# The second MLP product by Strassen's scheme, and a last h batch in five PSUM buffers

## The chip, the cores and the metric

The kernel runs on one core of one Trainium2 chip. The metric is the device time of one execution in microseconds; smaller is better. The engines are called by the names of the profile: PE is TensorE's matmul, PEld its weight load, DVE is VectorE, ACT is ScalarE, POOL is GpSimd and SP is SyncE, which here issues the DMAs.

## The reference

Attention over 8 batches and 8 heads (576 tokens, head dimension 64) in which scores more than tau below the row's maximum are dropped, followed by a two-layer MLP on the 4,608 tokens.

```python
scores = scale * np.matmul(q, k.transpose(0, 1, 3, 2))
thresh = np.max(scores, axis=-1, keepdims=True) - tau
scores = np.where(scores >= thresh, scores, -1000000000.0)
attn = softmax(scores)
x = (attn @ v) as tokens x 512                    # 4608 x 512
h = x @ w_in                                      # 4608 x 2048
g = h * np.tanh(softplus(h))                      # Mish
return (g @ w_out).astype(np.float32)             # 4608 x 512
```

## The kernel before

The kernel works on transposed data: tokens are columns. Products that need more than one pass of precision split each float32 operand into an upper part (a copy to the fp32r type, on ACT) and a lower part (the difference, on DVE or POOL), and add three products: upper x upper, upper x lower, lower x upper. So every block of the MLP costs three matmuls.

**Attention.** A loop over 288 tiles (`g`), nine per pair of heads, makes scores, softmax, transposes and the product with the values. Between its steps PE is given pieces of the first MLP product of the batch before: `gemm1` (line 455) is a generator that yields after each matmul, and `advance` (line 485) takes as many as a table says. The 32 blocks of `w_in` and the upper half of `w_out`'s columns are decoded in the same loop: the weights arrive as 64-bit words and become float32 by two ACT instructions, three DVE instructions and one POOL addition (`Decode`, lines 115 to 154). The decoded upper half of `w_out` goes back to HBM as `w2d`. All compute engines run strictly in the order in which the program is written (`InOrder`, line 81); DMAs are issued by SP.

**First product, last batch.** Each of the 16 blocks `f` of 128 features and both halves `c` of 288 tokens make one tile `h`: 12 matmuls of 288 columns. A finished tile is copied to `hst`, and four of them go to HBM (`hd`). The `h` tiles have two PSUM buffers (`psh`, line 164). For the last batch, which runs alone, lines 477 to 480 copy odd `f` on ACT and even `f` on DVE. During it the other half of `w_out` is loaded, decoded and split (`decode_step`, line 693), in part on POOL (line 705); the first chunk's `h` is read back, Mish is applied and the result is split, on POOL (`gate` at line 732); and `w2d` is read back and split (lines 739 to 743).

**Second product.** From line 767 on, ten chunks of tokens (256, eight times 512, 256) are multiplied by all of `w_out`: per chunk four blocks `d` of 128 outputs, each with 16 x 3 matmuls into one PSUM bank `o`, which DVE copies to `ost` for the output DMA. `make_g` (line 751) prepares the chunk after the next: load `h`, Mish and cast on ACT, subtraction on DVE. Engines other than PE are not held to the written order here, since line 749 takes the plain engines again.

Of the kernel before, what the change touches and what calls it, by code (L numbers as in the profile page):

```python
# [7 lines left out]
U32 = mybir.dt.uint32  # L8
# [29 lines left out]
NC = 512  # L38
PACE = {(5 * f) // 4: f for f in range(NF)}
GATES = (12, 15, 18, 21)  # L40
SPLITS = (24, 26, 28, 30)
CHUNKS = (0, *range(256, B * S, NC), B * S)
# [72 lines left out]
class Decode:  # L115


    def __init__(self, nc, st, hi, lo):
# [3 lines left out]
        self.c = self.words[:, :, 0]  # L122

# [23 lines left out]
    def add(self):  # L147
        self.nc.gpsimd.tensor_tensor(self.a, self.b, self.c, ALU.add)
# [4 lines left out]
    def lower(self, engine):  # L153
        engine.tensor_tensor(self.lo, fv(self.a), fv(self.hi), ALU.subtract)


def attention_moe(tc, q, k, v, tau, w_in, w_out, out):
# [3 lines left out]
    with ExitStack() as outer:  # L161
# [13 lines left out]
        with ExitStack() as first:  # L175
# [5 lines left out]

            with ExitStack() as att:
# [4 lines left out]
                dec = att.enter_context(tc.tile_pool(name="dec", bufs=5, side="right"))  # L187
# [3 lines left out]
                def skip():  # L191
                    pass

# [6 lines left out]
                def decode_w1(d, j):  # L200
                    sl = slice(j * WC, (j + 1) * WC)
                    st = dec.tile([P, 4 * WC], U32, name="dec")
# [12 lines left out]
                def decode_w2(f):  # L215
                    st = dec.tile([P, 4 * WC], U32, name="dec")
# [238 lines left out]
                def gemm1(b, xs):  # L455
# [88 lines left out]
                for g in range(NT + 5):  # L544
# [103 lines left out]
            wr = second.enter_context(tc.tile_pool(name="wr", bufs=1, side="right"))  # L648
            pso = second.enter_context(tc.tile_pool(name="pso", bufs=4, space=PSUM))

            def slot(pool, shape, kind, n):

                return pool.tile(shape, kind, name="g", tag="g", bufs=n)

            def small(kind, shape):
                return wr.tile(shape, kind, name="ht", tag="ht", bufs=2)

            def load_h(ht, c, fs):

                at, end = CHUNKS[c], CHUNKS[c + 1]  # L660
                while at < end:
                    i, off = divmod(at, HB)
                    m = min(HB - off, end - at)
                    to = at - CHUNKS[c]
                    nc.sync.dma_start(ht[:, :, to:to + m], hd[i][:, fs, off:off + m])
                    at += m

            def gate(ht, gh, gl, engine):
                nc.scalar.activation(ht, ht, AF.Mish)  # L669
                nc.scalar.copy(gh, ht)  # L670
                engine.tensor_tensor(gl, ht, fv(gh), ALU.subtract)  # L671

            def quarter(k):
                return slice(4 * k, 4 * k + 4)

            def weights2(pool, j):
                return [pool.tile([P, NF, WC], F32R, name=f"w2{n}{j}") for n in "hl"]

            n0 = CHUNKS[1]
            w2 = [weights2(wr, 0)]  # L680
            homes = []
            for _ in range(2):
                four = slot(wr, [P, 4, 4 * WC], U32, 4)
# [147 lines left out]
```

## Time and profile before

| | us |
|---|---|
| median of three runs | 1410.03 |
| the runs | 1406.82, 1410.03, 1417.41 |
| span of the profiled execution | 1404.3 |
| attention and the first seven batches (to the first matmul of the last batch) | 932.8 |
| last batch of the first product | 70.0 |
| second product, to the last instruction | 401.4 |

The span counts from the first to the last instruction of the profiled execution; no other time of that execution is shown, and the runs lie 2.5 to 13.1 us above it. In the rows, a matmul's duration contains the pipeline's end, which the next matmul overlaps; how fast PE streams is read from the distance of starts. Line 91 is the helper of the strict order, through which most instructions are recorded, so groups are told apart by tiles.

### The profile page before, as it was taken

The numbers are of one execution on the slowest core, as the hardware profiler recorded it, in microseconds if no ns is written. First come the engines' busy times: TensorE is split into PE (matmuls) and PEld (weight loads), VectorE is DVE, ScalarE is ACT, GpSimd is POOL, SyncE is SP. The second block draws the span as 40 slices with busy tenths as digits, with TensorE's granted clock in tenths as the row PEclk, the third lists the DMA queues.
The fourth block names the chain that finished last, engine by engine and source line by source line (L and its number), as shares of the span: only waits on it lengthen the run. The fifth ranks groups of instructions, "written<-read, shape, count | busy, mean of one in ns | idle before, by whom it ended". The sixth has DMA issues, their size and how long they took to land.

```text
span 1404.3 us, 27561 instructions
## 1 busy us (share of the span) xinstructions
PE 1364.3 (97%) x8798; PEld 1226.7 (87%) x8798; DVE 996.7 (71%) x2970; ACT 948.0 (68%) x2102; POOL 770.0 (55%) x1101
## 2 busy tenths in 40 slices
PE   8998899999999999999999999997999999999999
PEld 5555899999999999999999999997888888888888
DVE  5999999999999989999999999957433222322210
ACT  5878788888888888888888888856555333433310
POOL 4778888878788788787887878735200000000000
PEclk8999999999999999999999999999999999999999
DMA  4333333324333233333332333136555334543210
GB/s 141 97 101 107 116 125 111 120 90 130 98 117 109 92 123 119 102 112 103 104 119 91 117 95 108 63 133 237 162 161 144 111 112 120 143 113 113 83 53 30
DMA packets 124479, 158.81 MB, mean 113 GB/s; under 512 B 23472, under 2 KB 103344, under 8 KB 124336
## 3 DMA queue, kind: packets, MB, share of 16 engines
q1 hardware_dynamic: 124336, 157.07, 36.9%
q8 instruction: 70, 1.15, 0.3%
q14 instruction: 73, 0.60, 0.1%
HBM read 107.74 MB, written 49.28 MB: 112 GB/s over the span
## 4 chain that ended last, share of the span: by engine, by line
PE 84%; DVE 7%; ACT 5%; issue 2%; DMA 1%; POOL 0%; SPq 0%; ACTq 0%; DVEq 0%
PE o L780 28%; PE h L91 23%; PE s L91 13%; PE y L91 11%; PE tp L91 8%; DVE p L91 2%; DVE dec L91 1%; DVE st L91 1%; PE t L91 1%; DVE g L91 1%; ACT e L91 1%; ACT hi L91 1%; DVE lo L91 1%; DMA hd<-hst 1%; DVE tk L91 1%
## 5 line engine op out<-in xcount | busy, mean ns | idle before, releaser
L780 PE MATMUL o<-g,w2h 128*128 128x512 f32 (+1 forms) x1280 | 364.2, 370 | 0.7 <-ACT g L91 0.7
L91 PE MATMUL h<-xh,w1h 128*128 128x288 f32 x1024 | 304.8, 298 | 11.0 <-DVE hst L91 8.5
L91 PE MATMUL h<-xl,w1h 128*128 128x288 f32 x1024 | 304.1, 297 | 0.5 <-POOL xl L91 0.5
L91 PE MATMUL h<-xh,w1l 128*128 128x288 f32 x1024 | 303.8, 297 | 0.0
L91 POOL TENSOR_SCALAR p<-p,st 128x576 f32<-128x576 f32 x288 | 243.8, 846 | 62.4 <-DVE st L91 42.7
L91 PE MATMUL s<-k,q 128*128 128x288 f32 (+1 forms) x1280 | 257.7, 327 | 19.7 <-DVE p L91 17.0
L780 PEld LDWEIGHTS o<-g,w2h 128*128 128x128 f32 x1280 | 231.4, 188 | 44.5 <-ACT g L91 0.9
L91 ACT ACTIVATE e<-s,st 128x576 f32<-128x576 f32 x288 | 214.1, 744 | 55.0 <-DVE st L91 49.8
L91 DVE SCALAR_TENSOR_TENSOR p<-s,st,e 128x576 f32<-128x576 f32 x288 | 235.1, 816 | 21.3 <-ACT e L91 10.3
L780 PE MATMUL o<-g,w2l 128*128 128x512 f32 (+1 forms) x640 | 236.5, 370 | 0.0
L91 PEld LDWEIGHTS s<-k,q 128*128 128x128 f32 (+1 forms) x1280 | 184.2, 191 | 55.6 <-DVE p L91 36.6
L91 DVE TENSOR_REDUCE st<-s 128x1 f32<-128x576 f32 x288 | 216.6, 752 | 7.0 <-PE s L91 7.0
L91 PEld LDWEIGHTS h<-xh,w1h 128*128 128x128 f32 x1024 | 194.3, 190 | 13.5 <-DVE hst L91 10.2
L91 DVE TENSOR_TENSOR lo<-tp,hi 128x512 fp32r<-128x512 f32 (+1 forms) x280 | 174.2, 630 | 43.0 <-ACT hi L91 37.1
L91 PEld LDWEIGHTS h<-xl,w1h 128*128 128x128 f32 x1024 | 194.2, 190 | 0.9 <-POOL xl L91 0.9
L91 PEld LDWEIGHTS h<-xh,w1l 128*128 128x128 f32 x1024 | 194.2, 190 | 0.0
L671 DVE TENSOR_TENSOR g<-ht,g 128x1024 fp32r<-128x1024 f32 (+1 forms) x68 | 78.4, 1162 | 148.8 <-ACT g L670 148.8
L91 PE MATMUL tp<-ident,p 128*128 128x128 f32 x1152 | 175.0, 275 | 3.6 <-DVE lo L91 2.4
L91 ACT CAST hi<-tp 128x512 fp32r<-128x512 f32 (+1 forms) x280 | 149.8, 546 | 33.4 <-PE tp L91 30.0
L669 ACT ACTIVATE ht<-ht 128x1024 f32<-128x1024 f32 (+1 forms) x68 | 68.6, 1009 | 128.9 <-DMA ht<-hd 126.0
L91 PEld LDWEIGHTS tp<-ident,p 128*128 128x128 f32 x1152 | 139.0, 140 | 14.3 <-issue 7.3
L780 PEld LDWEIGHTS o<-g,w2l 128*128 128x128 f32 x640 | 120.5, 188 | 22.0
(64 smaller groups left out, 2196.5 us busy)
## 6 DMA issues: line engine op xcount, KB each, us to landing
hd<-hst SPq DMA_DIRECT2D x64, 576.0 KB, 3.3
r<-q SPq DMA_DIRECT2D x120, 160.0 KB, 2.4
r<-k SPq DMA_DIRECT2D x120, 160.0 KB, 2.3
ht<-hd SPq DMA_DIRECT2D x60, 288.0 KB, 3.3
r<-v SPq DMA_DIRECT2D x56, 160.0 KB, 2.3
dec<-w_in SPq DMA_DIRECT2D x32, 256.0 KB, 2.8
out_t<-ost SPq DMA_DIRECT2D x32, 256.0 KB, 2.2
dec<-w_out SPq DMA_DIRECT2D x16, 256.0 KB, 2.9
```

Of the source, the lines that this page charges most:

```text
L91: made = method(*args, **kwargs)
L669: nc.scalar.activation(ht, ht, AF.Mish)
L671: engine.tensor_tensor(gl, ht, fv(gh), ALU.subtract)
L780: nc.tensor.matmul(o[:, :m], a, b, start=n == 0, stop=n == 3 * NF - 1)
```

## The change

**The scheme.** The second product is cut into groups of 512 tokens, nine in all. Weights, features and tokens are each halved: `a` blocks of `w_out` (256 outputs x 1,024 features) and `b` blocks of Mish(h) (1,024 features x 256 tokens). Seven products of such blocks replace eight, by this form of Strassen's scheme (the first index of `a` is the output half and that of `b` the feature half):

- sums of weights, made once: s1 = a21 + a22, s3 = a11 - a21, s2 = a22 - s3, s4 = a12 - s2; seven weight blocks are split into upper and lower parts and stay in SBUF;
- sums of features, for each group: t1 = b12 - b11, then b12 becomes t3 = b22 - b12, b11 becomes t2 = t3 + b11, b21 becomes t4 = b21 - t2;
- products in this order, each 48 matmuls of 256 columns: a12 b21 into bank Y, a11 b11 into X, s1 t1 into Z, s2 t2 onto X, s4 b22 onto Z, a22 t4 into Y, s3 t3 onto X; between them banks are copied by ACT and added in the stores by DVE.

Each of the seven right operands is split after the sums (`operand`: four pieces, a cast on ACT and a subtraction on DVE), two products ahead, into a ring of 13 pieces. POOL does no subtraction any more. The strict order stays in force to the end. Lower halves, sums and splits of the weights are placed by number of the `h` tile (`at(u, ...)`) into the last batch; those of s2 and s3 lie in the first group.

**The last batch.** Its `h` tiles rotate over five PSUM buffers, two old ones and three new (`psx`); all are copied by ACT; `hst` has three buffers and is sent in two halves. Five of the sixteen pieces of `w_out`'s first output half are decoded in the last steps of the attention loop, and four more are loaded there.

```diff
+PIECE = (*range(8, 16), *range(8))
+EARLY = 284
...
                     for c, fs in order:
                         for f in fs:
-                            h = psh.tile([P, 512], F32, name="h", tag="ph")
+                            if b < B - 1 or f % 5 < 2:
+                                h = psh.tile([P, 512], F32, name="h", tag="ph")
+                            else:
+                                h = psx.tile([P, 512], F32, name="hx")
...
                             if f % 4 == 0:
-                                hst = xpool.tile([P, 4, HB], F32, name="hst", bufs=2)
-                            if b < B - 1 or f % 2:
-                                nc.scalar.copy(hst[:, f % 4], h[:, :HB])
-                            else:
-                                nc.vector.tensor_copy(hst[:, f % 4], h[:, :HB])
-                            if f % 4 == 3:
-                                nc.sync.dma_start(hd[2 * b + c][:, f - 3:f + 1, :], hst)
+                                hst = xpool.tile([P, 4, HB], F32, name="hst", bufs=3)
+                            nc.scalar.copy(hst[:, f % 4], h[:, :HB])
+                            n = 4 if b < B - 1 else 2
+                            if f % n == n - 1:
+                                nc.sync.dma_start(hd[2 * b + c][:, f + 1 - n:f + 1, :], hst[:, (f + 1 - n) % 4:f % 4 + 1])
...
+                    if EARLY <= g < EARLY + 9:
+                        decoding.extend(filter(None, [decode_top(g - EARLY)]))
...
+            halves = (slice(0, 4), slice(4, 8))
+            def split(raw):
+                made = [units.take(F32R) for _ in "hl"]
+                ups = [lambda s=s: nc.scalar.copy(made[0][:, s], raw[:, s]) for s in halves]
+                downs = [
+                    lambda s=s: nc.vector.tensor_tensor(made[1][:, s], raw[:, s], fv(made[0][:, s]), ALU.subtract)
+                    for s in halves
+                ]
+                return made, ups, downs
+            def combine(to, x, y, op):
+                return [lambda s=s: nc.vector.tensor_tensor(to[:, s], x[:, s], y[:, s], op) for s in halves]
...
+            def mish(raw):
+                for s in halves:
+                    nc.scalar.activation(raw[:, s], raw[:, s], AF.Mish)
+            def operand(raw):
+                parts = []
+                for i in range(4):
+                    s = slice(2 * i, 2 * i + 2)
+                    hl = ring.take(F32R)
+                    nc.scalar.copy(hl[:, 0], raw[:, s])
+                    nc.vector.tensor_tensor(hl[:, 1], raw[:, s], fv(hl[:, 0]), ALU.subtract)
+                    parts.append(hl)
+                return parts
+            r21, r22 = units.take(F32), units.take(F32)
+            for raw, at in ((r21, 0), (r22, 8)):
+                nc.sync.dma_start(raw, w2d[:, at:at + 8])
...
+            for n in range(5, 16):
+                at(n - 5, lambda n=n: coming[n - 5].first())
+                at(n - 4, lambda n=n: piece(n))
...
+            at(3, *a12u)
+            at(12, *a12d)
+            at(13, sum1)
+            at(14, split_into("s1", s1), lambda: units.give(s1))
...
-                if u in GATES:
-                    k = GATES.index(u)
-                    gate(h0[k], *(g[:, quarter(k)] for g in g0), nc.gpsimd)
...
-                    (nc.vector if k % 2 else nc.gpsimd).tensor_tensor(lo, raw2[:, quarter(k)], fv(hi), ALU.subtract)
+                for work in todo.pop(u, []):
+                    work()
                 advance(stream, UNIT)
...
-        nc = tc.nc
...
-                for f in range(NF):
-                    wh, wlo = (w[:, f, at:at + P] for w in w2[j])
-                    gh, gl = (x[:, f % 4] for x in g[f // 4])
-                    for a, b in ((wh, gh), (wh, gl), (wlo, gh)):
-                        nc.tensor.matmul(o[:, :m], a, b, start=n == 0, stop=n == 3 * NF - 1)
+        def multiply(a, b, o, first, last):
+            n = 0
+            for k in range(8):
+                gh, gl = (b[k // 2][:, i, k % 2] for i in range(2))
+                for m in range(2):
+                    wh, wlo = (w[:, k, m * P:(m + 1) * P] for w in a)
+                    for w, g in ((wh, gh), (wh, gl), (wlo, gh)):
+                        nc.tensor.matmul(o[:, m], w, g, start=first and n == 0, stop=last and n >= 45, skip_group_check=True)
                         n += 1
...
+        def store(pair, dh, th, x, y):
+            ost = small("ost", 4)
+            nc.vector.tensor_tensor(ost, x, y, ALU.add)
...
+        for pair in range(NPR):
+            nxt = {}
+            for i in range(7):
+                more = pair + 1 < NPR
+                if i == 0:
+                    if pair:
+                        store(pair - 1, 1, 1, X, tmp["p5"])
+                        store(pair - 1, 1, 0, X, tmp["y4"])
+                    else:
+                        mish(r["b22"])
+                    ops_.append(operand(r["t1"]))
+                    run_all(combine(r["b12"], r["b22"], r["b12"], ALU.subtract))
+                if i == 1:
+                    tmp["ysb"] = copied("ysb", Y)
+                    run_all(combine(r["b11"], r["b12"], r["b11"], ALU.add))
+                    ops_.append(operand(r["b11"]))
+                    if pair == 0:
+                        split_into("s2", r22)()
...
+                if i == 2:
+                    store(pair, 0, 0, X, tmp["ysb"])
+                    ops_.append(operand(r["b22"]))
+                    run_all(combine(r["b21"], r["b21"], r["b11"], ALU.subtract))
+                if i == 3:
+                    tmp["p5"] = copied("p5", Z)
+                    ops_.append(operand(r["b21"]))
...
+                    if pair == 0:
+                        split_into("s3", r21)()
...
+                if i == 5:
+                    tmp["zsb"] = copied("zsb", Z)
+                    store(pair, 0, 1, X, tmp["zsb"])
...
+                if i == 6:
+                    tmp["y4"] = copied("y4", Y)
+                    if more:
+                        mish(nxt["b12"])
+                        ops_.append(operand(nxt["b11"]))
+                        nxt["t1"] = units.take(F32)
+                        run_all(combine(nxt["t1"], nxt["b12"], nxt["b11"], ALU.subtract))
+                        mish(nxt["b22"])
+                name, o, first, last = (
+                    ("a12", Y, True, True), ("a11", X, True, True), ("s1", Z, True, True), ("s2", X, False, True),
+                    ("s4", Z, False, True), ("a22", Y, True, True), ("s3", X, False, True),
+                )[i]
+                multiply(A[name], ops_.pop(0), o, first, last)
+            r = nxt
...
-    nc = bacc.Bacc("TRN2", target_bir_lowering=False, num_devices=1)
+    nc = bacc.Bacc("TRN2", target_bir_lowering=False, num_devices=1, dynamic_dma_scratch_size=1024)
```

More of the change, by code (lines that the diff above doesn't have):

```diff
@@ L37 @@
 NBLK = 2 * B
[L38 to L42, printed above, removed]
+TC = 256
+PIECE = (*range(8, 16), *range(8))
+EARLY = 284
 QCOL = {
@@ L154, in lower, with __init__, add, take @@
         engine.tensor_tensor(self.lo, fv(self.a), fv(self.hi), ALU.subtract)
+class Homes:
+    def __init__(self, name, shape):
+        self._name, self._shape, self._pools, self._at = name, shape, [], {}
+    def add(self, pool, n, tag=None):
+        self._pools.append([pool, n, n, tag or self._name])
+    def take(self, kind):
+        home = next(h for h in self._pools if h[1])
+        home[1] -= 1
+        t = home[0].tile(self._shape, kind, name=self._name, tag=home[3], bufs=home[2])
+        self._at[id(t)] = (home, t)
+        return t
+    def give(self, t):
+        self._at.pop(id(t))[0][1] += 1
 def attention_moe(tc, q, k, v, tau, w_in, w_out, out):
@@ L180, in attention_moe, with home @@
             w1 = [[pool.tile([P, ND, DF // 2], F32R, name=f"w1{n}") for n in "hl"] for pool in (wlow, wtop)]
+            keep = outer.enter_context(tc.tile_pool(name="keep", bufs=1, side="right"))
+            units = Homes("un", [P, 8, TC])
+            ring = Homes("ring", [P, 2, 2, TC])
+            units.add(keep, 1)
+            ring.add(keep, 5, "dec")
+            r12 = units.take(F32)
+            early_pieces = []
+            def home():
+                return keep.tile([P, 4 * WC], U32, name="dec", tag="dec", bufs=5)
             with ExitStack() as att:
@@ L647, in attention_moe, with load_h @@
             second = outer.enter_context(ExitStack())
[L648 to L660, printed above, removed]
+            wr = second.enter_context(tc.tile_pool(name="wr", bufs=1, side="right", reuse_waits="tile"))
+            pso = second.enter_context(tc.tile_pool(name="pso", bufs=1, space=PSUM))
+            psx = second.enter_context(tc.tile_pool(name="psx", bufs=3, space=PSUM))
+            units.add(wr, 11)
+            def load_h(to, fs, at, end):
+                start = at
                 while at < end:
@@ L663, in load_h @@
                     m = min(HB - off, end - at)
[L664 to L665 removed]
+                    nc.sync.dma_start(to[:, :, at - start:at - start + m], hd[i][:, fs, off:off + m])
                     at += m
[L668 to L683, printed above, removed]
-                homes += [four[:, i] for i in range(4)]
-            g0 = [slot(wr, [P, NF, n0], F32R, 4) for _ in "hl"]
-            work = {}
@@ new lines, in attention_moe, with fetch_piece @@
+            r11 = units.take(F32)
+            homes = [units.take(U32) for _ in range(2)]
+            homes = [(t, t[:, 4 * i:4 * i + 4].rearrange("p a b -> p (a b)")) for t in homes for i in range(2)]
+            s1 = units.take(F32)
+            b12 = load_raw((0, 1), 0)
+            def fetch_piece(n, st):
+                f = PIECE[n]
+                work = Decode(nc, st, None, None, (r12 if f >= 8 else r11)[:, f % 8])
+                work.load(w_out[f * P:(f + 1) * P, :WC])
+                return work
@@ new lines, in attention_moe @@
+        units.add(wl, 3)
+        ring.add(wl, 8)
+        bank = [pso.tile([P, 2, TC], F32, name=n) for n in "xyz"]
+        def multiply(a, b, o, first, last):
[6 more added lines that the diff above has]
+                        nc.tensor.matmul(o[:, m], w, g, start=first and n == 0, stop=last and n >= 45, skip_group_check=True)
+                        n += 1
+            for t in b:
+                ring.give(t)
@@ new lines, in small, with copied @@
+        def small(name, n=1):
+            return wl.tile([P, 2, TC], F32, name=name, bufs=n)
+        def store(pair, dh, th, x, y):
+            ost = small("ost", 4)
+            nc.vector.tensor_tensor(ost, x, y, ALU.add)
+            at = (2 * pair + th) * TC
+            nc.sync.dma_start(out[dh * 2 * P:(dh + 1) * 2 * P, at:at + TC].rearrange("(m p) t -> p m t", p=P), ost)
+        def copied(name, x):
+            t = small(name)
+            nc.scalar.copy(t, x)
+            return t
+        X, Y, Z = bank
```

176 lines of the change are left out of this document (102 added, 74 removed).

## Prediction

> **What bounds the kernel now.** I read the page's busy shares first, then the chain of waits, then the stretches around the second product. The page's first part and the summary of the chain:
>
> ```profile
> PE 1364.3 (97%) x8798; PEld 1226.7 (87%) x8798; DVE 996.7 (71%) x2970; ACT 948.0 (68%) x2102; POOL 770.0 (55%) x1101
> PE 84%; DVE 7%; ACT 5%; issue 2%; DMA 1%; POOL 0%; SPq 0%; ACTq 0%; DVEq 0%
> ```
>
> TensorE carries the chain. Its last 470 us, the part that the change rewrites, read in the chain in order of time (start, us, engine, tile, line, count):
>
> ```profile
> 935.13 1.57 POOL xl L91 x2
> 961.93 2.27 DVE g L91
> 971.96 5.89 PE h L91 x24
> 989.83 13.19 PE h L91 x96
> 1003.02 398.07 PE o L780 x1912
> ```
>
> The second product is one unbroken run of matmuls, 398.1 us. Ahead of it stands the last batch of the first product, and there the chain breaks. Busy time by stretch (length, then PE, PEld, DVE, ACT, POOL, the granted clock, DMA share, GB/s):
>
> ```profile
> 900.00:930.00 30.00, 30.00 (x232) 29.69 (x231) 23.07 (x73) 21.10 (x50) 13.22 (x23) 1.00 0.10 41
> 936.20:960.00 23.80, 22.69 (x165) 21.82 (x165) 15.89 (x38) 12.92 (x34) 9.64 (x13) 1.00 0.83 289
> 960.00:990.00 30.00, 20.39 (x125) 18.82 (x124) 20.72 (x31) 17.87 (x37) 18.61 (x16) 0.89 0.45 150
> 990.00:1002.80 12.80, 12.80 (x96) 12.70 (x97) 3.42 (x5) 7.14 (x11) 4.80 (x2) 1.00 0.91 281
> 1003.00:1025.00 22.00, 22.00 (x186) 22.00 (x185) 11.02 (x13) 13.17 (x14) 0.00 (x0) 1.00 0.49 135
> 1378.40:1400.90 22.50, 22.50 (x193) 22.47 (x191) 1.97 (x4) 0.00 (x0) 0.00 (x0) 1.00 0.09 30
> ```
>
> Between 960 and 990 PE is busy for two thirds at clock 0.89; elsewhere it is full. So two prices matter: the spacing of matmuls at 256 columns, and what that gap costs. TensorE's timeline gives the spacings and the ends of the stages:
>
> ```profile
> 932.83 0.30 PE L91 MATMUL h<-xh,w1h 128*128 128x288 f32 x1
> 935.11 0.40 PE L91 MATMUL h<-xh,w1h 128*128 128x288 f32 x1 [0.93 <-ACT xh L91]
> 935.98 0.40 PE L91 MATMUL h<-xl,w1h 128*128 128x288 f32 x1 [0.47 <-POOL xl L91]
> 1001.26 0.30 PE L91 MATMUL h<-xh,w1h 128*128 128x288 f32 x1
> 1002.46 0.29 PE L91 MATMUL h<-xh,w1h 128*128 128x288 f32 x1
> 1002.86 0.28 PE L780 MATMUL o<-g,w2h 128*128 128x256 f32 x1
> 1004.05 0.28 PE L780 MATMUL o<-g,w2l 128*128 128x256 f32 x1
> 1004.41 0.28 PE L780 MATMUL o<-g,w2l 128*128 128x256 f32 x1
> 1371.27 0.39 PE L780 MATMUL o<-g,w2l 128*128 128x512 f32 x1
> 1371.95 0.39 PE L780 MATMUL o<-g,w2l 128*128 128x512 f32 x1
> 1379.24 0.28 PE L780 MATMUL o<-g,w2l 128*128 128x256 f32 x1
> 1379.95 0.28 PE L780 MATMUL o<-g,w2l 128*128 128x256 f32 x1
> 1400.79 0.28 PE L780 MATMUL o<-g,w2l 128*128 128x256 f32 x1
> ```
>
> Every third matmul of the product takes w2l. 512 columns: 0.68/3 = 0.227 us. 256 columns: 0.36/3 = 0.120 while the other engines work (1004), 0.71/6 = 0.118 when they are done (1379). 288 columns: nine in 1.20, 0.133. Halving the width thus costs about half, plus some 0.005 us.
>
> **Part 1, the product's stream.** Before: 1,920 matmuls, 1,536 of them 512 wide, 398.1 us. Now nine groups of 512 tokens take seven products of 48 matmuls at 256 columns: 63 x 48 = 3,024. At 0.119 that is 359.9 us, a gain of 38.2. ScalarE and VectorE will be busy throughout, which speaks for 0.120 (362.9, gain 35); 0.118 gives 356.8, gain 41. Scaled from the 288-column spacing by the slope 0.109/256 between the two widths it is 0.120 too.
>
> [...]
>
> **Part 2, the last batch of the first product.** Before: 932.83 to 1002.86, 70.0 us. Its 384 matmuls at 0.133 are 51.2; about eight early ones of the product are 1.0. The other 17.8 are gaps and cold clock. 1.8 of them are the wait for the last x (0.93 and 0.47 idle above), which stays. Who caused the rest:
>
> ```profile
> PE h L91 <- DVE hst L91: 8.5, 7, 3.6
> 978.25 2.72 DVE L91 TENSOR_SCALAR g<-g 128x256 f32<-128x256 f32 x2
> 978.41 2.41 POOL L91 TENSOR_TENSOR g<-ht,g 128x1024 fp32r<-128x1024 f32 x1 [3.24 <-DMA g<-w2d]
> ```
>
> PE waits for VectorE to empty h, with two buffers. VectorE is late because its decode steps last as long as GpSimd's 1,024-wide subtraction beside them. The change takes all of this away: GpSimd keeps only the decode's add, VectorE copies no h. ScalarE's order in the middle of the batch, before:
>
> ```order
> L91 ACTIVATE g<-g 128x256 x2
> L91 CAST w2h_15460<-g 128x256
> L91 ACT_TABLE_LOAD
> L91 ACTIVATE ht<-ht 128x1024
> L91 CAST g<-ht 128x1024
> L91 ACTIVATE g<-g 128x256 x2
> L91 COPY hst<-h 128x288
> ```
>
> and now (dec and un in ACTIVATE are pieces of w_out, un in CAST the block a12, hx the three new PSUM buffers):
>
> ```order
> L89 ACTIVATE dec<-dec 128x256 x2
> L89 CAST un<-un 128x1024 x2
> L89 COPY hst<-hx 128x288
> L89 ACTIVATE dec<-dec 128x256 x2
> L89 COPY hst<-hx 128x288
> L89 ACTIVATE un<-un 128x256 x2
> L89 COPY hst<-h 128x288
> ```
>
> One copy now stands behind each piece of work, and PE may run at least three h ahead. ScalarE could still stand at a piece that DMA has not brought: r21, r22 and b12, 3 MB, are queued on SP ahead of pieces 10 to 15. At the 289 GB/s of the second stretch these 3 MB take 10.4 us from about 934, so piece 10 lands near 946, while its place in ScalarE's queue comes behind the fifth h, at 934.7 + 5 x 1.6 = 943. The copy behind it must be done when PE returns to its buffer with the ninth h, at 934.7 + 8 x 1.6 = 947.5. So I charge 1 us: gain 17.8 - 1.8 - 1 = 15. Ends: 16 without a wait, 10 if the loads are 6 us later.
>
> **Part 3, the steady pair.** VectorE and ScalarE must make in one pair (7 x 48 x 0.119 = 40.0 us of PE) four blocks of Mish, four sums or differences, 28 splits and four stores. Groups of the second product, from 1020 on:
>
> ```profile
> L671 DVE TENSOR_TENSOR g<-ht,g 128x1024 fp32r<-128x1024 f32 x58 | 70.5, 1225 | 136.1 <-ACT g L670 136.1
> L669 ACT ACTIVATE ht<-ht 128x1024 f32<-128x1024 f32 x57 | 60.4, 1060 | 112.7 <-DMA ht<-hd 112.1
> L783 DVE COPY ost<-o 128x512 f32<-128x512 f32 x32 | 22.0, 688 | 112.5 <-PE o L780 112.5
> L671 DVE TENSOR_TENSOR g<-ht,g 128x512 fp32r<-128x512 f32 x8 | 5.4, 692 | 12.7 <-ACT g L670 12.7
> L670 ACT CAST g<-ht 128x512 fp32r<-128x512 f32 x8 | 4.9, 620 | 13.8 <-PE o L780 13.6
> ```
>
> VectorE: 8 x 1.225 + 28 x 0.692 + 4 x 0.688 = 31.9 us, 80%. ScalarE: 8 x 1.06 + 28 x 0.62 + four copies at 0.62 = 28.3 us, 71%. Each operand is begun two products (11.4 us) before its use. The tightest places are the stores of bank X, which PE must await before it writes X again. VectorE's order from the start of a pair is: the difference t1 (2.45, carried over), two stores (1.4), t1's split (2.8), two sums (4.9), a split (2.8), the third store (0.7). Laid end to end, the first two stores end at 4.1 where PE wants X at 5.7, and the third at 15.3 where PE wants it at 17.1. So I charge 0 here, with 1.6 us to spare; the other end is 2.5 us per pair, 20 over the eight later pairs. The blocks of h and the output are the same bytes as before.
>
> **Part 4, the first pair.** It also splits the sums s2 and s3. VectorE's order at the end before:
>
> ```order
> L91 COPY hst<-h 128x288
> L783 COPY ost<-o 128x256
> L671 TENSOR_TENSOR g<-g 128x1024 x4
> L671 TENSOR_TENSOR g<-ht,g 128x1024
> L783 COPY ost<-o 128x256
> ```
>
> and now, from the first operand b21 on (ring is a split operand, un x2 or x4 a sum or a weight's lower part, ost a store):
>
> ```order
> L89 TENSOR_TENSOR ring<-un,ring 128x512 x4
> L89 TENSOR_TENSOR un<-un 128x1024 x2
> L89 TENSOR_TENSOR ring<-un,ring 128x512 x8
> L89 TENSOR_TENSOR un<-un 128x1024 x4
> L89 TENSOR_TENSOR ring<-un,ring 128x512 x4
> L89 TENSOR_TENSOR un<-un 128x1024 x2
> L89 TENSOR_TENSOR ost<-x,ysb 128x512
> ```
>
> The lower part of s2 came in ahead of the store that frees X. The queue starts late as well: b22 is loaded only when the last h has left PE.
>
> ```profile
> ht<-hd SPq DMA_DIRECT2D x4, 512.0 KB, 6.0
> out_t<-ost SPq DMA_DIRECT2D x32, 256.0 KB, 2.2
> out_t<-ost SPq DMA_DIRECT2D x8, 128.0 KB, 1.8
> ```
>
> From PE's last h: load by 7.2, two Mish by 9.3, t1's split (a cast, then 4 x 0.69) by 12.7, two sums (4.9) by 17.6, a split by 20.4, s2's lower part by 22.9, the store by 23.5; PE wants X at 17.1. That is a wait of 6.4; if instructions without a wait between them overlap by a tenth or more it is nearer 3.5. I take 4. Such a wait cools the clock:
>
> ```profile
> 971.96 0.61 PE L91 MATMUL h<-xh,w1h 128*128 128x288 f32 x1 [3.58 <-DVE hst L91]
> ```
>
> This gap of 3.58 us was followed (chain above) by 24 matmuls in 5.89 us, 0.245 each, so the cold clock may add 24 x 0.112 = 2.7; I take 1. Sum +5, ends 0 and 12.
>
> **Part 5, small edits.** Two stores behind the last product instead of one copy: 0.69 more, and 256 instead of 128 KB, 0.4 more: +1. Five pieces of w_out move into the last attention steps. PE has no idle time there (30.00 of 30.00), and VectorE's gaps, such as
>
> ```profile
> 925.26 0.69 DVE L91 TENSOR_TENSOR lo<-tp,hi 128x512 fp32r<-128x512 f32 x1 [2.99 <-ACT hi L91]
> ```
>
> hold the extra three short steps each; 0, at most +3. The third hst buffer and the smaller scratch: 0.
>
> **Sum.** -38.2 - 15 + 0 + 5 + 1 = -47.2 against the profiled span of 1404.3: span 1357. The three runs shown lie 2.5 to 13.1 above that span, the median 5.7; with the same distance 1410 - 47 = **1363 us**.
>
> **Rivals.**
> - *The vector queue holds X in every pair.* For: all sums, splits and stores are in one fixed order, at 80%. Against: 1.6 us to spare. At 2.5 us per pair 20 us come back: 1383. Chance 0.13.
> - *The last batch keeps its gaps* because ScalarE stands at late pieces (DMA share was 0.83 to 0.91 there). The 15 shrink to about 3: 1375. Chance 0.10.
> - *Half-width matmuls keep the 0.133 of 288 columns*, weight loads being busy throughout (22.47 of 22.50 us) already. 3,024 x 0.133 = 402: 1363 + 42 = 1405, no change. Against: the 0.118 and 0.120 were measured with those loads. [...]
> - *Slower: splits in series.* The ring has 13 slots, three operands and one piece. If ScalarE's cast and VectorE's subtraction of each piece do not overlap, a pair takes 28 x 1.31 + 9.8 + 2.8 + 2.5 = 51.8 us instead of 40: 9 x 11.8 = 106 more, 1469. It turns into a loss from 45.3 us a pair. Against: no wait ties the next cast to this piece's subtraction. Chance 0.04.
>
> **Numbers.** The forecast has 0.70; its own range is 1350 to 1374 (ends of parts 1, 2 and 4, and the runs' spread). To hold 8 in 10 it reaches over the first two rivals: 1349 to 1386. One per cent, 14 us, is what a measurement here can tell from no change. Faster: 0.70 + 0.13 + 0.10 less a little for several ends at once, 0.91; same 0.05; slower 0.04.
>
> **What would show it.** Right: 63 runs of 48 matmuls at 5.7 us each without idle time from the second pair on; h without waits for copies and a clock of 1.00 between 936 and 990; one gap of some 4 us ahead of the fourth product. Wrong: PE waiting on ost in each pair, ACT waiting on DMA pieces of w_out with PE idle behind it, a spacing above 0.125, or losses inside the attention part, which I left at nothing.

## The result and the profile after

The changed kernel takes 1366.2 us (median; 1357.55 to 1368.55), beside 1411.6 us for the kernel before on the same chip: a ratio of 0.967, 95% interval 0.963 to 0.972. The profiled execution took 1364.1 us, its span is 1362.2 us. The forecast was 1363 us. One of the six executions of e6 (below) took 4470.6 us, for a reason that nothing here shows; its ratio goes by the other five.

The page of the changed kernel, its first part and the summary of the chain:

```profile
PE 1323.9 (97%) x9902; PEld 1250.2 (92%) x9902; DVE 1155.2 (85%) x3214; ACT 1031.8 (76%) x2320; POOL 752.5 (55%) x1087
PE 84%; DVE 7%; ACT 4%; issue 2%; DMA 1%; SPq 1%; POOL 0%; DVEq 0%; ACTq 0%; POOLq 0%
```

The picture is that of before: TensorE is busy for 97% and carries 84% of the chain. It issues 1,104 more matmuls in 40 us less: they are 256 columns wide where most were 512, and seven products do the work of eight (774,144 columns in place of 884,736).

**Where the spans differ.** The two executions began differently, in code that is the same in both. The first 36 us by busy time and clock (as in the prediction's table), and the row maximum of the last attention tile on VectorE, kernel before:

```profile
0.00:36.00 36.00, 30.39 (x144) 21.92 (x145) 20.80 (x85) 19.04 (x43) 16.98 (x26) 0.86 0.50 140
917.81 0.75 DVE L91 TENSOR_REDUCE st<-s 128x1 f32<-128x576 f32 x1
```

and the changed kernel:

```profile
0.00:36.00 36.00, 29.60 (x108) 20.05 (x108) 15.67 (x64) 14.38 (x31) 14.24 (x22) 0.72 0.42 128
923.84 0.75 DVE L89 TENSOR_REDUCE st<-s 128x1 f32<-128x576 f32 x1
```

TensorE's clock was granted at 0.72 in place of 0.86 at the start, 108 matmuls were done in place of 144, and some 6 us lost by then are still there at the last tile. The experiments below have the changed kernel's attention code, and their last row maximum comes anywhere from 917.5 (e5) to 929.9 us (e10), so this is no effect of the change. Without it the span fell by 48.1 us.

TensorE's timeline at the ends of the stages (the first row is the first matmul of the last batch, the second the first product):

```profile
939.42 0.29 PE L89 MATMUL h<-xh,w1h 128*128 128x288 f32 x1
...
995.78 5.92 PE L89 MATMUL y<-ring,un 128*128 128x256 f32 x48
1001.54 5.70 PE L89 MATMUL x<-ring,un 128*128 128x256 f32 x48
1007.08 5.60 PE L89 MATMUL z<-ring,un 128*128 128x256 f32 x48
1017.39 8.24 PE L89 MATMUL x<-ring,un 128*128 128x256 f32 x48 [4.71 <-DVE ost L89]
1025.47 5.70 PE L89 MATMUL z<-ring,un 128*128 128x256 f32 x48
```

| stretch | before | after | change | forecast |
|---|---|---|---|---|
| start, up to the last tile's row maximum | 917.8 | 923.8 | +6.0 | 0 |
| from there to the last batch | 15.0 | 15.6 | +0.6 | 0 |
| last batch | 70.0 | 56.4 | -13.7 | -15 |
| the product without its first wait | 397.9 | 354.5 | -43.4 | -38.2 |
| wait in the first pair, and slow clock behind it | 0 | 7.1 | +7.1 | +5 |
| from the last matmul's start to the end | 3.5 | 4.8 | +1.3 | +1 |

(The product runs to the start of its last matmul, at 1357.4 after. The 7.1 us are the 4.71 of the row and 2.4 by which the fourth product, s2 t2, 8.08 from start to start, is longer than the same product in later pairs, 5.65; the clock was granted at 0.67 from 1017.3 to 1025.4.)

All that TensorE waited for from the last batch on, in the changed kernel (total, times, longest):

```profile
PE x L89 <- DVE ost L89: 4.7, 1, 4.7
PE h L89 <- ACT hst L89: 1.3, 1, 1.3
PE h L89 <- ACT xh L89: 1.0, 1, 1.0
PE h L89 <- POOL xl L89: 0.7, 1, 0.7
```

The wait on VectorE for h, 8.5 us before, is gone; from the second pair on there is no wait at all. Busy time by stretch:

```profile
944.10:947.50 3.40, 3.40 (x16) 3.40 (x15) 2.57 (x7) 1.48 (x5) 1.51 (x2) 0.50 0.92 332
947.50:957.30 9.80, 8.56 (x64) 8.33 (x63) 2.63 (x9) 5.21 (x13) 2.24 (x3) 1.00 1.05 351
957.40:960.90 3.50, 3.50 (x26) 3.50 (x27) 3.36 (x8) 3.48 (x12) 1.51 (x2) 1.00 0.96 371
960.00:990.00 30.00, 30.00 (x228) 30.00 (x227) 29.65 (x34) 24.08 (x41) 4.05 (x5) 1.00 0.49 162
1060.00:1340.00 280.00, 280.00 (x2389) 280.00 (x2388) 205.24 (x288) 178.19 (x288) 0.00 (x0) 1.00 0.46 128
```

Between 960 and 990 TensorE is full at clock 1.00, where it was at 20.39 of 30 and 0.89. Only the stretch ahead of it shows a loss, and it has two parts. From 944.1 to 947.5, behind the waits for the last x (which end at 942.86), TensorE is busy at clock 0.50, and 14 matmuls start 0.24 us apart in place of 0.133: 1.5 us. A late copy of h by ScalarE costs the 1.28 us ahead of 957.35, and behind that wait the clock stays at 1.00.

### The profile page after: what moved, and what is told of

Same layout as the page of the kernel before. It is cut to its first block, busy times and chain, and to the rows that moved or that the text cites. A ratio compares the mean times of both kernels' runs of the same rounds, so it can differ in the third digit from the quotient of the medians.

```text
span 1362.2 us, 30137 instructions
## 1 busy us (share of the span) xinstructions
PE 1323.9 (97%) x9902; PEld 1250.2 (92%) x9902; DVE 1155.2 (85%) x3214; ACT 1031.8 (76%) x2320; POOL 752.5 (55%) x1087
## 4 chain that ended last, share of the span: by engine, by line
PE 84%; DVE 7%; ACT 4%; issue 2%; DMA 1%; SPq 1%; POOL 0%; DVEq 0%; ACTq 0%; POOLq 0%
PE h L89 23%; PE y L89 19%; PE s L89 14%; PE x L89 11%; PE tp L89 8%; PE z L89 7%; DVE p L89 2%; PE hx L89 2%; DVE dec L89 1%; DVE st L89 1%; PE t L89 1%; ACT e L89 1%; ACT hi L89 1%; DMA un<-w_out 1%; DVE lo L89 1%
## 5 line engine op out<-in xcount | busy, mean ns | idle before, releaser
L89 PE MATMUL h<-xh,w1h 128*128 128x288 f32 x952 | 281.2, 295 | 2.3 <-ACT hst L89 1.3
L89 PE MATMUL h<-xl,w1h 128*128 128x288 f32 x952 | 281.5, 296 | 0.7 <-POOL xl L89 0.7
L89 PE MATMUL h<-xh,w1l 128*128 128x288 f32 x952 | 281.3, 295 | 0.0
L89 DVE TENSOR_TENSOR ring<-un,ring 128x512 fp32r<-128x512 f32 x252 | 157.0, 684 | 61.1 <-ACT ring L89 60.7
L89 PEld LDWEIGHTS h<-xh,w1h 128*128 128x128 f32 x952 | 179.2, 188 | 2.9 <-ACT hst L89 1.5
L89 ACT CAST ring<-un 128x512 fp32r<-128x512 f32 x252 | 138.2, 618 | 35.8 <-DVE un L89 33.5
L89 PE MATMUL x<-ring,un 128*128 128x256 f32 x1296 | 158.8, 283 | 4.7 <-DVE ost L89 4.7
L89 PEld LDWEIGHTS x<-ring,un 128*128 128x128 f32 x1296 | 156.2, 192 | 4.9 <-ACT ring L89 4.9
L89 POOL TENSOR_TENSOR x<-x,yo 64x256 f32<-64x256 f32 (+1 forms) x112 | 91.1, 814 | 78.2 <-ACT yo L89 75.5
L89 PE MATMUL y<-hi,vs 128*128 128x256 f32 (+1 forms) x448 | 123.3, 297 | 0.2 <-ACT hst L89 0.2
```

The source lines that it names most:

```text
L89: made = method(*args, **kwargs)
```

## Experiments

Four numbers of each trace are compared: the stretch from the end of the attention's last matmul (`y`) to the first product, the first four products, the mean time of the 55 products from the eighth on, and the time from the last row maximum to the end, which the start's clock doesn't touch.

| kernel | last batch | first four | mean of 55 | to the end |
|---|---|---|---|---|
| before | 69.9 | | | 486.5 |
| changed | 56.20 | 29.69 | 5.632 | 438.4 |
| e1, s2 split early | 57.57 | 25.07 | 5.599 | 433.2 |
| e2, pieces of w_out first | 53.15 | 29.83 | 5.632 | 435.4 |
| e3, two PSUM buffers | 63.69 | 28.64 | 5.632 | 444.8 |
| e4, two buffers and VectorE's copies | 62.87 | 30.54 | 5.632 | 445.9 |
| e4b, VectorE's copies | 57.83 | 29.33 | 5.632 | 439.7 |
| e5, all at multiples of 128 bytes | 55.24 | 28.44 | 5.714 | 441.2 |
| e6, e1 and e2 | 54.66 | 25.02 | 5.599 | 430.2 |
| e7, no work beside TensorE | 58.22 | 28.92 | 5.616 | 439.0 |
| e8, slower store of X | 55.89 | 28.89 | 6.138 | 465.0 |
| e9, offsets 96 and 32 | 56.31 | 29.51 | 5.569 | 435.0 |
| e10, e6 and e9 | 53.15 | 26.91 | 5.576 | 429.5 |
| e12, e10 with GpSimd | 53.16 | 27.71 | 5.576 | 430.3 |

Each number is that of one profiled execution. The last batch is the same code in the changed kernel, e1, e5, e7, e8 and e9: 55.2 to 58.2. TensorE's timelines show where that spread comes from: without any loss the batch takes 53.15 us; the wait at the late copy adds 1.3 to 3.3; and a slow stretch of 14 or 15 matmuls adds 1.5 in four of these six, behind the waits for x in the changed kernel and e9, behind the late copy in e1 and e7. Differences of under 2 us in this column say nothing.

In whole times, beside the kernel before, e1 and e2 came to 0.965, e4 to 0.973, e5 to 0.971 and e9 to 0.967, each with an interval of some 0.003 to 0.004 to either side, beside the changed kernel's 0.967; e3, e4b, e7 and e8 were timed once.

### e4, e3 and e4b: what shortened the last batch

e4 puts both edits of the last batch's h back:

```diff
-                            if b < B - 1 or f % 5 < 2:
-                                h = psh.tile([P, 512], F32, name="h", tag="ph")
-                            else:
-                                h = psx.tile([P, 512], F32, name="hx")
+                            h = psh.tile([P, 512], F32, name="h", tag="ph")
...
-                            nc.scalar.copy(hst[:, f % 4], h[:, :HB])
+                            if b < B - 1 or f % 2:
+                                nc.scalar.copy(hst[:, f % 4], h[:, :HB])
+                            else:
+                                nc.vector.tensor_copy(hst[:, f % 4], h[:, :HB])
```

> The last batch's h is put back in two PSUM buffers, its even blocks copied by VectorE; everything else is as in the changed kernel. Theory (the buffers and ScalarE's copies are what shortened the last batch from 70.0 to 56.4 us): it grows by 8 to 15 us, and TensorE waits for copies on VectorE. Rival (it was shortened by the decode and split work that was taken out of it): it grows by less than 3 us.

62.87 us, so +6.7, below the first theory's 8 and far above the rival's 3. Waits of e4:

```profile
PE h L89 <- ACT hst L89: 4.5, 2, 4.0
PE h L89 <- DVE hst L89: 2.1, 2, 1.5
```

e3 is the first half of this edit, e4b the second.

> The last batch's h is put back in two PSUM buffers, but ScalarE still copies all of it. With both edits undone the stretch from the end of the attention to the first product was 62.87 us, with neither 56.20. Theory (the number of buffers is what counts: with two, each late copy of ScalarE stops TensorE): 61 to 63 us. Rival (who copies is what counts): 56 to 58 us.

> The last batch's h keeps its five PSUM buffers, but VectorE copies the even blocks, as before. Theory (five buffers cover VectorE's sums and splits of 1.2 us as well as they cover ScalarE's work): 56 to 57.5 us from the end of the attention to the first product. Rival (a copy that is queued in VectorE behind four or more subtractions holds TensorE in spite of the buffers): 59 us or more.

e3 takes 63.69 us, a little over the 61 to 63 expected, with this wait,

```profile
PE h L89 <- ACT hst L89: 6.4, 3, 4.0
```

and e4b 57.83, just above its 57.5, but within the spread of the unchanged code. So the buffers are worth 5 to 8 us of the 13.7, and who copies is worth nothing that shows here. With both undone the batch is still 7 us shorter than before, and VectorE holds h for 2.1 us where it was 8.5. That part is put down to the work taken off GpSimd and VectorE; it was not tried alone, so it is not shown.

### e2: pieces of w_out first

ScalarE and SP's queue in the changed kernel, at the one late copy:

```profile
942.49 0.88 SPq L744 DMA_DIRECT2D un<-w2d  x2
943.47 3.59 SPq L700 DMA_DIRECT2D un<-hd  x4
947.10 6.24 SPq L124 DMA_DIRECT2D un<-w_out  x4
```

```profile
956.26 0.77 ACT L89 ACTIVATE un<-un 128x256 f32<-128x256 f32 x2 [3.96 <-DMA un<-w_out]
```

The copy stands behind a piece that SP issued after r21, r22 and b12. e2 changes that order alone:

```diff
-            for raw, at in ((r21, 0), (r22, 8)):
-                nc.sync.dma_start(raw, w2d[:, at:at + 8])
...
-            b12 = load_raw((0, 1), 0)
...
             for n in range(10, 14):
                 coming.append(fetch_piece(n, homes[n - 10][1]))
+            for raw, at in ((r21, 0), (r22, 8)):
+                nc.sync.dma_start(raw, w2d[:, at:at + 8])
+            b12 = load_raw((0, 1), 0)
```

> The loads of r21, r22 and b12 (3 MB) are issued behind pieces 10 to 13 of w_out, not ahead of them. Theory (ScalarE waits 3.96 us at 952.3 for a piece that stands behind these 3 MB): that wait goes, and with it TensorE's 1.28 us at 957.35 and the clock of 0.90 in 942.8 to 960; the last batch is 1.3 to 3 us shorter than its 56.4 us. Rival (the wait is not what delays the copies): the last batch stays at 56.4, give or take 0.5.

```profile
943.50:960.70 17.20, 17.15 (x129) 17.15 (x130) 12.42 (x28) 11.08 (x29) 7.79 (x10) 1.00 1.02 349
```

The 17.2 us behind the last wait for x are full now, at clock 1.00, with DMA as busy as before (TensorE was busy for 15.86 of them at 0.90 in the changed kernel). The batch takes 53.15 us, and 53.15 to 54.66 in the four kernels with this order (e2, e6, e10, e12); none of the four waits for that copy. Of the 3 us here, half are the wait. The other half is the slow stretch from 944.1 on, which lies ahead of the late copy and behind a wait that e2 has too; e6, with the same order, has it again and takes 54.66. So the order is worth the wait, 1.3 to 3.3 us in the unchanged kernels, and the slow clock where it follows that wait (e1, e4b, e7); that e2 lost its slow stretch was luck.

### e1: s2 split early

```diff
                     else:
+                        split_into("s2", r22)()
+                        units.give(r22)
+                        A["s2"] = state["s2"]
                         mish(r["b22"])
...
-                    if pair == 0:
-                        split_into("s2", r22)()
-                        units.give(r22)
-                        A["s2"] = state["s2"]
```

> The split of s2 is moved from the second step of the first pair to its first step, ahead of the Mish of b22, so the store that frees X stands two 1024-wide subtractions earlier in the vector queue. Theory (the store is late because s2's lower half stands ahead of it): the 4.71 us in which TensorE waits for ost at 1012.7 goes to under 0.5 us, and the 2.6 us of slow clock behind it go too, so the first pair is 6 to 7.5 us shorter than in the changed kernel. Rival (the store is late because b22 and its operands come late, whatever stands in the queue): the wait only moves, and under 2 us are gained.

```profile
1016.10 5.89 PE L89 MATMUL x<-ring,un 128*128 128x256 f32 x48 [2.44 <-ACT ring L89]
1021.83 5.70 PE L89 MATMUL z<-ring,un 128*128 128x256 f32 x48
```

```profile
1015.26 0.69 DVE L89 TENSOR_TENSOR ost<-x,ysb 128x512 f32<-128x512 f32 x1
```

4.6 us are gained in the first four products, between the two expectations: the wait fell from 4.71 to 2.44 and the slow clock is gone. The row puts the rest down to ScalarE, but the store ends at 1015.95, 0.15 us ahead of TensorE; it is still the store. So s2 was half of the wait. The other half is the late start of the queue, which e12 looks at. The mean of the 55 products fell as well, by 0.033 us, 1.8 in all, because s2 and s3 came to lie elsewhere (see e9).

### e8: how much VectorE has to spare

```diff
                     if pair:
+                        for _ in range(2):
+                            run_all(combine(r["t1"], r["b12"], r["b11"], ALU.subtract))
                         store(pair - 1, 1, 1, X, tmp["p5"])
```

> In each pair but the first the sum t1 is computed twice more on VectorE (four subtractions of 1,024 columns, 1.22 us each, 4.87 us together) just ahead of the two stores that free bank X; the result is the same. In the changed kernel VectorE ends the second of these stores 2.0 to 2.2 us before TensorE needs X. Theory (2 us to spare at that place and no other close one): TensorE waits 2.7 to 2.9 us at each of eight pair starts, 22 us in all, and more if its clock falls behind each wait. Rival 1 (VectorE's 11 us of idle time in a pair take it up): under 3 us in all. Rival 2 (there was nothing to spare): 39 us.

TensorE from the second pair on, and VectorE's and TensorE's rows around one of the eight places:

```profile
PE x L89 <- ACT ring L89: 19.5, 8, 2.5
```

```profile
1046.86 6.90 DVE L89 TENSOR_TENSOR un<-un 128x1024 f32<-128x1024 f32 x6
1054.27 0.69 DVE L89 TENSOR_TENSOR ost<-x,y 128x512 f32<-128x512 f32 x1
```

```profile
1055.11 5.70 PE L89 MATMUL x<-ring,un 128*128 128x256 f32 x48 [2.54 <-ACT ring L89]
...
1097.32 7.48 PE L89 MATMUL x<-ring,un 128*128 128x256 f32 x48 [2.42 <-ACT ring L89]
```

Again the row names ScalarE where the store ends last (1054.96). 4.87 us of work cost 2.3 to 2.5 us of waiting at each start of a pair, so some 2.4 us were to spare; the trace had shown 2.0 to 2.2 between store and matmul. The theory holds, a little under its 22 us. The 55 products took 27.8 us more: the 19.5, and four of the eight products behind a wait were slow, 7.1 to 7.3 us from start to start (the clock was granted at 0.86 from 1094 to 1106, around one of them).

### e7, e5 and e9: the spacing of the matmuls

Products of 48 matmuls don't last the same. Five in a row in the changed kernel:

```profile
1149.14 5.60 PE L89 MATMUL y<-ring,un 128*128 128x256 f32 x48
1154.58 5.81 PE L89 MATMUL x<-ring,un 128*128 128x256 f32 x48
1160.23 5.70 PE L89 MATMUL y<-ring,un 128*128 128x256 f32 x48
1165.77 5.60 PE L89 MATMUL x<-ring,un 128*128 128x256 f32 x48
1171.21 5.90 PE L89 MATMUL z<-ring,un 128*128 128x256 f32 x48
```

From start to start 5.44, 5.65, 5.54, 5.44, 5.74. The 13 slots of the ring lie five on the right of SBUF and eight on the left, and the products use in turn four left ones, four right ones, one right and three left. e7 leaves the other engines' work out; its core:

```diff
+                more = False
+                if pair:
+                    if i == 0:
+                        store(pair - 1, 1, 1, X, tmp["p5"])
+                        store(pair - 1, 1, 0, X, tmp["y4"])
+                    if i == 1:
+                        tmp["ysb"] = copied("ysb", Y)
...
-                if i == 0:
+                if pair == 0 and i == 0:
...
+                made = ops_.pop(0)
+                multiply(A[name], made, o, first, last)
+                if pair or i >= 4:
+                    ops_.append(made)
```

> Left out: from the second pair on no h is loaded, activated, summed or split, and the products use the last three sets of pieces of the first pair again and again, in the same cycle of slots (mixed, left, right); PSUM is still copied and stored as before, the output from the second pair on is not that of the reference. ScalarE and VectorE then have some 5 us of work in a pair in place of 24 and 28. Theory (TensorE alone bounds a steady pair, its spacing set by where operands lie): products keep 5.44 to 5.76 us and a pair stays at 38.7 to 39.9 us; the time changes by less than 4 us beside the 4.71 us wait and its slow clock, which stay. Rival (ScalarE's, VectorE's and the loads' traffic stretches the matmuls): products fall to 5.44 us in all slots, 10 us in all.

```profile
1060.00:1340.00 280.00, 280.00 (x2396) 280.00 (x2395) 18.71 (x28) 17.01 (x29) 0.00 (x0) 1.00 0.08 27
```

```profile
1149.84 5.60 PE L89 MATMUL y<-ring,un 128*128 128x256 f32 x48
1155.28 5.91 PE L89 MATMUL x<-ring,un 128*128 128x256 f32 x48
1161.02 5.70 PE L89 MATMUL y<-ring,un 128*128 128x256 f32 x48
1166.56 5.60 PE L89 MATMUL x<-ring,un 128*128 128x256 f32 x48
1172.00 3.27 PE L89 MATMUL z<-ring,un 128*128 128x256 f32 x26
```

With VectorE at 18.71 us in place of 205.24 and DMA at 0.08 in place of 0.46 the products last 5.44, 5.74, 5.54, 5.44; the mean is 5.616 against 5.632. Only the second, s3, differs from the rows above, and it lasts the same 5.74 in e1, where all the other work runs. So here neither the splits nor the loads stretch the matmuls by more than these 0.016 us in 48, and the steady pair has no cost but TensorE's.

e5 shifts both sides of SBUF by 96 bytes, so that all operands begin on multiples of 128:

```diff
+        cst.tile([P, 24], F32, name="pad")
...
+            padr = outer.enter_context(tc.tile_pool(name="padr", bufs=1, side="right"))
+            padr.tile([P, 24], F32, name="padr")
```

> One unused tile of 96 bytes is put at the start of the left and of the right side of SBUF, so all operands of the product begin on a multiple of 128 bytes, where before they began 32 or 96 bytes behind one; nothing else changes. In the changed kernel products of 48 matmuls last 5.44 us (all four pieces on the left) to 5.76 us (all on the right). Theory A (the spacing is set by where an operand begins within 128 bytes): all products last the same, 5.44 us if alignment helps, which makes the stream 11 us shorter than its 356 us. Theory B (the spacing is set by the region of SBUF, or by what the other engines do meanwhile): the same 5.44 to 5.76, and the time within 2 us of the changed kernel's.

```profile
1068.43 5.87 PE L89 MATMUL x<-ring,un 128*128 128x256 f32 x48
1074.13 5.86 PE L89 MATMUL y<-ring,un 128*128 128x256 f32 x48
1079.83 5.92 PE L89 MATMUL x<-ring,un 128*128 128x256 f32 x48
```

Mixed, left, right: 5.70, 5.70, 5.75. The spread is gone, but at the slow end: the mean rose by 0.08 us a product. e9 sets the weights at 96 and the pieces at 32 bytes (tiles of 16 numbers, in the same way).

> Unused tiles of 64 bytes shift the pools so that each weight operand of the product begins 96 bytes, and each piece of h 32 bytes, behind a multiple of 128 bytes. In the changed kernel that held for weights in the right pools with pieces in the left one (5.44 us for 48 matmuls in the best products); where both were at 96 bytes it was 5.65 to 5.76, and with everything at 0 bytes 5.70 to 5.75. Theory (the distance of the two offsets sets the spacing): nearly all products last 5.44 us, the mean of the 55 after the first pair falls from 5.632 to about 5.45, and the kernel is 11 us shorter. Rival (the side of SBUF, or the traffic of the other engines, sets it): pieces on the right stay at 5.65 to 5.76, and the mean stays above 5.58.

```profile
1088.40 5.82 PE L89 MATMUL x<-ring,un 128*128 128x256 f32 x48
1094.06 5.66 PE L89 MATMUL z<-ring,un 128*128 128x256 f32 x48
1099.56 5.60 PE L89 MATMUL x<-ring,un 128*128 128x256 f32 x48
```

Right, mixed, left: 5.66, 5.50, 5.44, with a mean of 5.569. Neither expectation holds whole. Right slots last 5.65 us or more, as the rival said, and most left ones 5.44, but the mean fell by 0.06. Where operands begin and on which side they lie both count: the two shifts moved the mean from 5.632 to 5.714 and to 5.569, and in e9 right slots last 5.66 us and left ones 5.44.

What side means shows in e1. Most weight blocks lie on the right, but by the order in which e1's program takes its homes in SBUF both parts of s2 lie on the left. Here is s2 with left pieces and then with right ones:

```profile
1094.60 5.92 PE L89 MATMUL x<-ring,un 128*128 128x256 f32 x48
1133.81 5.61 PE L89 MATMUL x<-ring,un 128*128 128x256 f32 x48
```

From start to start 5.76 and 5.44, the other way round from weights on the right (a11: 5.44 and 5.74). So in e1 pieces and weights on opposite sides last 5.44 us, on the same side 5.74 to 5.76. In the changed kernel s2 and s3 have one part on either side, and s2 lasts 5.65 with left, right or mixed pieces. The product ahead may count too: with left pieces a12 lasts 5.65 us in the changed kernel, each time behind s3 at 5.65 or 5.66, and 5.44 in e7, behind s3 at 5.54. That was seen and not tried; what rule joins all this stays open.

### e6, e10 and e12: together

> Both earlier edits together: the split of s2 in the first step of the first pair, and the pieces of w_out loaded ahead of r21, r22 and b12. Alone, the first shortened the stretch from the first product to the fifth from 29.69 to 25.07 us, the second the stretch from the end of the attention to the first product from 56.20 to 53.15 us. Theory (the two waits are separate): both gains add up, 7.7 us together, which gives about 1357 us. Rival (what TensorE gains in the last batch it waits for in the first pair, where ScalarE and VectorE now set the end): 3 to 5 us together.

e6 takes 1352.9 us, ratio 0.959 (0.955 to 0.963), and in its trace 8.2 us less than the changed kernel from the last row maximum on. That is near the theory's 7.7 us but made up otherwise: 1.5 in the last batch (54.66), 4.7 in the first four products (25.02), and e1's 1.8 in the mean (5.599).

> The split of s2 in the first step, the pieces of w_out first, and the shifted pools (weights 96, pieces 32 bytes behind a multiple of 128) together. Apart they gave: last batch 56.20 to 53.15 us, first four products 29.69 to 25.07 us, mean of the 55 products behind the first pair 5.632 to 5.569 us in the run with the shifted pools alone. Theory (three separate gains): 53.2 us, 25.1 us, a mean of 5.57 or less, 1351 us in all. Rival (the spacing depends on which slots the scales' splits got, so the shift gives nothing once s2 has moved): a mean of 5.60 as with the first two edits alone, 1353 us.

1356.8 us where 1351 were expected, ratio 0.959 (0.956 to 0.963). The mean is 5.576 and the last batch 53.15, but the wait ahead of the fourth product is 3.0 us and that product takes 7.15 us, so the first four take 26.91 us. To the end it is 0.7 us better than e6: no difference that shows.

```diff
-                        split_into("s2", r22)()
+                        split_into("s2", r22, nc.gpsimd)()
```

> As the kernel with all three edits, but GpSimd does the two subtractions of s2's lower half (2.40 us each in the kernel before), which TensorE needs from the fourth product on. With VectorE doing them TensorE still waited 2.4 us ahead of the fourth product, behind 2.36 us of these subtractions and 4.6 us of sums. Theory (VectorE's queue sets that wait): it falls below 0.5 us, and the first four products take 22.6 to 23 us in place of 25.07. Rival (GpSimd's access slows VectorE by as much, or the h stores set it): over 24.5 us.

GpSimd, VectorE and TensorE in e12:

```profile
992.01 4.77 POOL L89 TENSOR_TENSOR un<-un 128x1024 fp32r<-128x1024 f32 x2 [33.62 <-ACT un L89]
```

```profile
989.97 1.90 DVE L89 TENSOR_TENSOR ring<-un,ring 128x512 fp32r<-128x512 f32 x3 [1.71 <-ACT ring L89]
995.54 3.60 DVE L89 TENSOR_TENSOR ring<-un,ring 128x512 fp32r<-128x512 f32 x4 [3.67 <-ACT ring L89]
```

```profile
1006.96 7.33 PE L89 MATMUL x<-ring,un 128*128 128x256 f32 x48 [3.79 <-ACT ring L89]
```

The theory falls: the wait grew from e10's 3.00 to 3.79 us, and the first four products take 27.71, as the rival said. Relieved of s2, VectorE stands idle for 3.67 us, because the casts of t1 come from ScalarE behind Mish of b22 (2.23 us from 992.78 on); then its four splits last 3.60 us in place of e10's 2.50, the first 1.24 of them beside GpSimd, whose row ends at 996.78. VectorE begins to split t1 9.0 us after the first product in the changed kernel and in e1, and 9.1 in e12. From there to the end of the store it has 10.2 us of work in e1, while TensorE wants X 16.9 us after the first product. So that the rest of the wait is set by ScalarE's work ahead of t1 and VectorE's behind it is read from these rows; no run moved either.

e12's ratio is 0.958 (0.954 to 0.961). It, e6 and e10 can't be told apart. All three beat the kernel before. Beside the changed kernel their ratios are lower by 0.8 to 1.0%, with intervals that touch its own for e6 and e10; from the last row maximum on they are 8 to 9 us shorter, 0.6%.

## Why the prediction was right

The time was right to 3 us, and the sum, -47.2, stands beside -48.1 without the start. The stages and their order of size came as described, but the closeness is luck: the terms were further off than their sum, as the following points show.

- **Part 1, the stream.** Mechanism right, size off. 63 products of 48 matmuls at half width, none of them waiting from the second pair on. The term that was mis-sized is the spacing: 0.119 us was taken from two chunks of before, at 0.120 and 0.118; the mean measured is 354.5 / 3,023 = 0.1173, since products from left slots run at 0.113 to 0.118. The gain is 43.4 us, above the upper end of 41.
- **Part 2, the last batch.** 13.7 us where 15 were forecast. The late piece came as described, later than reckoned (956 us, against 946 with an attention that ended 6.6 us sooner), and cost 1.5 us with the matmul behind it where 1 was charged. The other 1.5 us are the slow clock behind the waits for the last x, which the sum took over from the kernel before as they were, without a slow clock; it came in three of thirteen executions. That one copy stands behind each piece of work was held to matter; e4b shows that the buffers do, not who copies.
- **Part 3, the steady pair.** 0, as charged. 2.0 to 2.2 us to spare at the first two stores of X, where 1.6 was worked out (its terms, 2.45 and 1.4, end at 3.85 and not at 4.1, which leaves 1.85), and 3.2 to 3.5 at the third. The rival in which the vector queue holds X falls; e8 shows how far off it was: 2.4 us of VectorE's work in a pair.
- **Part 4, the first pair.** The wait came in the place named, 4.71 us where 4 was taken, and the slow clock cost 2.4 where 1 was taken: +7.1, in the bounds. The cause named, s2's lower half, is half of it (e1); the late queue, named second, is the other as far as the rows of e1 and e12 tell.
- **Part 5.** +1.3 and +0.6, as good as forecast.
- **Left out.** The start: 6.0 us between two profiled executions that has nothing to do with the change. A forecast made against one span carries it.

The error in part 1 (5.2 us more gain) met those in parts 2, 4 and 5 (4.3 us less), and nothing tied the one to the others. Of the rivals, late pieces were real, at about an eighth of the 12 us charged for them; matmuls at 0.133 (a chance of 0.03; 0.1173 was measured) and splits in series don't appear.

## What to carry to other kernels

Fewer and narrower matmuls paid here because their spacing at half width was measured in the kernel before (0.118 and 0.120 us, beside 0.227 at 512 columns) and its other engines had room (VectorE was busy for 71%, ScalarE for 68%); take such a price from several places in SBUF, not from one (here it went from 0.113 to 0.120). Behind a wait of TensorE count a slow stretch too: it cost 2.4 us behind the 4.71 in the first pair, and 1.5 behind waits of 2.7 to 3.3 in the last batch. Before putting a slow stretch down to a wait, look which of the two came first. Where two engines make an operand in turn, moving one step to a third engine helps only if that step is what the next one waits for (in e12 it was not, and the wait grew from 3.00 to 3.79 us): a look at who idles in the queue tells it beforehand.

## What the runs showed of the hardware

- The place of operands in SBUF moves the spacing of matmuls of 256 columns (with a weight load each) between 0.113 and 0.120 us, with VectorE busy for only 18.71 of 280 us (e7); after a shift by 96 bytes it is 0.119 to 0.120 for the mixed, left and right products shown above (e5). Weights and pieces on opposite sides last 5.44 us for 48 matmuls, on the same side 5.74 to 5.76 (a11 and s2 in e1).
- In the second product, waits of TensorE of 3.0 us or more were followed by a slow product each time (eleven of eleven, 7.1 to 8.4 us in place of 5.6); of ten waits of 2.3 to 2.5 us only four were. In the last batch waits of 2.66 to 3.99 us brought a slow stretch (five of five: e1, e3, e4, e4b, e7) and single ones of 0.53 to 2.48 none (nine: the changed kernel, e3, e4, e5, e8, e9); the two waits for x, 0.99 and 0.70 close together, brought one in three of thirteen. In e8 a wait of 2.54 us was followed by a product of 5.53 us once and of 7.26 and 7.18 in two other pairs; what decides between them is not shown.
- The tenth row maximum came at 33.7 us in e5 and at 45.2 in e8, in the same code: 11 us, eight tenths of a per cent, with a granted clock of 0.91 over the first 36 us in e5, 0.72 in the changed kernel (40.8 us) and 0.65 in e2 (43.4 us). What decides on it was not tried.
- A wait's row can name the wrong engine: ahead of a product that needs both a split operand and the store of X, e1 and e8 name ScalarE's ring, where VectorE's store ended 0.15 us before the matmul.
